# A fused attention and gated-MLP kernel: one more unit of score tiles early, the output projection spread over 36 steps

## The chip, the cores and the metric

The kernel runs on one core of a Trainium2 chip. Its engines are TensorE (PE, with PEld for its weight loads), VectorE (DVE), ScalarE (ACT), GpSimd (POOL) and SyncE (SP), which issues most DMAs. The metric is the device time of one execution in microseconds (us). All floats are 32 bits wide.

## The reference

With 2048 tokens, model width 512, 32 heads of 16 and a hidden width of 1376, the program computes

```
xn = layernorm(x)
q, k, v = split(xn @ wqkv)                      # 32 heads of 16
s = softmax(q @ k.T / 4) @ v                    # per head
s = concat_heads(s) @ wo
g = gelu_tanh(xn @ w1 + b1) @ w2 + b2
out = x + s * silu(g)
```

## The kernel before, in words

Most products are made of three matmuls of a rounded high part and a low remainder (`mm3`, and `i, j` in `terms`). The work has two parts.

**The dense part** makes xn, v, q, k and the MLP. Its matmuls are cut to 64 rows, so that two run beside each other on the two 64-row halves of TensorE ("row tiles", `a` = 0 and 1). `run` issues them alternately and calls `fill` ahead of each. `fill` adds score tiles. A score tile is 128 queries by 512 keys of one head: one matmul of 48 rows (`s_mm`, L193) into a PSUM bank, and one row maximum by DVE (`s_max`, L199). The maxima are wanted because the second pass subtracts them inside its matmul. `fill` makes a tile whenever the count of dense matmuls (`row`) has reached `2 * FILL0 + APART * (tiles made)`, until `SOON` tiles are made. In the dense part the tiles use two banks in turn (`s_ring = [ps_a, ps_b]`), so each tile waits for the maximum of the tile but one before it. A unit is one group of four heads by 512 queries, 64 tiles; when it ends, DVE makes `nm` from its maxima (L255), every second time with a transpose (L244).

POOL makes the low parts (`w_split`, and `hl` at L375, which the second MLP product reads). Its `chore` adds b2 to a finished MLP tile and sends it to DRAM (`g_d`).

**The attention loop** has 32 units of 16 steps, 512 steps and a last one. A step makes the transposed scores of 128 keys by 512 queries for four heads ("T", `t_one`, L716: 4 matmuls of 50 rows on the two row tiles, into banks of `ps_m`, `two`, `two` and `ps_t`), their exponentials on ACT (L719 and L721), and the product with V of the step before ("V", `pv_step`, L787: 4 matmuls on column tiles, each executed as two). Between them stand two or three of the remaining score tiles (letters S, X, Y of `ORDER`; here three banks are in the ring). The letters give TensorE's order by hand. `due(n)` says how many tiles are made by step n; `FEW` takes some away, one each 16 steps until it is used up.

From step `DONE` on no score tile is left. The order `TWO` then holds "H", the projection with Wo of two token tiles (`w_halves`, L916, 6 matmuls of 64 rows on both row tiles, 8 such halves for a pair of token tiles, into two banks of the ring), and "W" (`w_out`): DVE multiplies the finished projection with the gate (`w_gate`, L922), POOL adds x and the result leaves. V is issued for two steps at once there. A token tile's gate is loaded (`load_gx`) and made by a tanh on ACT (L850) and a DVE instruction (L851). After the loop the last six token tiles are projected.

K of a group of four heads lies in one of three sets (`g % KB`); a set is loaded again (`load_k`, on POOL's queue) when its group is done. Units are taken group after group, four chunks of 512 queries each.

Of the kernel before, what the change touches and what calls it, by code (L numbers as in the profile page):

```python
# [16 lines left out]
P = 128  # L17
# [18 lines left out]
DONE = 493  # L36
FILL0 = 2
APART = 5
# [4 lines left out]
TWO = ("HTTTTHWV", "TTTTHHV")  # L43
SOON = 590
FEW = 17
# [3 lines left out]
KB = 3  # L49
XB = 6  # L50
# [4 lines left out]
def fused(ctx: ExitStack, tc: tile.TileContext, x, wqk, wv, wo, w1, b1, w2, b2, out):  # L55
# [45 lines left out]

    s_ring = [ps_a, ps_b]
# [11 lines left out]
    def load_k(g, pieces=range(6), eng=nc.sync, c0=0, n=S):  # L114
        both = kws[g % KB]
        for i in pieces:
            a, b = divmod(i, 3)
            r, cs = slice(64 * a + DH * b, 64 * a + DH * b + DH), slice(c0, c0 + n)
            src = rows((qk_h, qk_h, qk_l)[b], g, 1, a, c0, n)
            if both is not None:  # L120
                eng.dma_start(both[r, :, cs].bitcast(F32), src)
            else:
                for p in range(2):
                    eng.dma_start(kts[g % KB][p][r, cs].bitcast(F32), src[:, p])

# [15 lines left out]
    def q_rows(qs, u, sides=range(2)):  # L141
        g, c = divmod(u, NCH)
# [39 lines left out]
    def at_of(job):  # L182
        u, st, p = job
        return divmod(st, NCH) if u % (NCH * KB) else divmod(st, NCH)[::-1]

    def s_mm(ps, job, a, c0, k0, w):
        u, st, p = job
        qi, ki = at_of(job)
        if u not in MX:
# [4 lines left out]
                                kts[u // NCH % KB][p][r, k0:k0 + w], start=True, stop=True).ins  # L194
# [364 lines left out]
    def fill(a):  # L559
        due = 2 * FILL0 + APART * sum(made)  # L560
        if sum(made) < SOON and row[0] >= due and (made[0] <= made[1]) == (a == 0):
# [4 lines left out]
            s_one(a)  # L566
# [86 lines left out]

    def chore():
# [50 lines left out]
    def t_one(u, k, i, pair=False):  # L705
        g = u // NCH
# [9 lines left out]
        nc.tensor.matmul(ps, kts[g % KB][p][r, k * P:(k + 1) * P],  # L716
# [7 lines left out]
    for n, e in enumerate(plan):  # L724
# [17 lines left out]
        if e[0] == "half" and pairs[e[1]][0] == ("q", NG - 1, 0) and e[2] == 1:  # L742
            kts.append([slot(p, (P, S), F32R) for p in range(2)])
            kws.append(None)
            qss.append(slot(2, (P, 2, 2, CH), F32R))
            ask_k(2)
# [3 lines left out]
    while errands:  # L750
        errand()
    assert sum(made) == SOON
# [12 lines left out]
    wo_h = kp.tile([P, KT, D], F32R, name="wo_h")  # L765
    wo_l = kp.tile([P, KT, D], F32R, name="wo_l")

    WR = {}

    def load_wo(k):  # L770
        WR[k] = wb.tile([P, 2, D], F32, name="gx", bufs=4)[:, 0]
        nc.sync.dma_start(WR[k], wo[k * P:(k + 1) * P, :])

    def wo_high(k):
        nc.gpsimd.tensor_copy(wo_h[:, k], WR[k])

    def wo_low(k):
        nc.gpsimd.tensor_sub(wo_l[:, k], WR.pop(k), wo_h[:, k].bitcast(F32))

    PV, OS, DN, DR = {}, {}, {}, {}  # L780
    def pv_step(u, k):
        g = u // NCH
# [16 lines left out]
    def o_rows(u, j):  # L799
        g, c = divmod(u, NCH)  # L800
# [23 lines left out]
    def o_div(u, eng):  # L824
        g, c = divmod(u, NCH)
# [5 lines left out]
    def home(i):  # L831
        if i not in homes:
            homes[i] = (slot(i, (P, KT, D)) if i < KB else
                        keep_r.tile([P, 2 * KT, D], F32, name="kt0"))
        return homes[i]

    def load_gx(t):
        i = 2 * (t % NCH)
        if t < NW - 2:
            GX[t] = wb.tile([P, 2, D], F32, name="gx", bufs=4)  # L840
        elif t < NT - NCH:
            GX[t] = home(KB)[:, i:i + 2]
# [34 lines left out]
    def w_mul(t, ks, parts=(0, 1)):  # L877
# [4 lines left out]
        for i, cs in enumerate(cols(t)):  # L882
            if i in parts:
                for k in ks:
                    mm3(PW[t][i][:, :cs.stop - cs.start], OTS[t, k], (wo_h[:, k, cs], wo_l[:, k, cs]),
                        k == 0, k == KT - 1)

    def w_two(t, k0):
# [4 lines left out]
        if t:  # L893
            nc.scalar.activation(hi, src, AF.Copy)
        else:
            nc.gpsimd.tensor_copy(hi, src)
# [7 lines left out]
    def w_halves(t, k, side):  # L904
# [7 lines left out]
        for n, (x, y) in enumerate(((0, 0), (0, 1), (1, 0))):  # L912
            for a in range(2):
                i = ts[a ^ side]
                r = slice(64 * a, 64 * a + 64)
                HALF[0] = nc.tensor.matmul(PW[i][0], OTS[i, k][x][r], (wo_h, wo_l)[y][r, k],  # L916
# [27 lines left out]

    for u in range(NU):
        g, c = divmod(u, NCH)
        if c == 0 and g == KB:
            for i in range(6):
                at(52 + i // 2, load_k, g, (i,), nc.gpsimd, 0, CH)
                at(56 + i // 2, load_k, g, (i,), nc.gpsimd, CH, CH)  # L950
                at(64 + i // 2, load_k, g, (i,), nc.gpsimd, S // 2, S // 2)
        elif c == 0 and g > KB:
            for i in range(6):
                at(64 * (g - KB + 1) + 6 + i, load_k, g, (i,), nc.gpsimd)
# [13 lines left out]
    for t in range(NW):  # L968
        n = DONE + 4 * (t // 2)
        at(n - 3 + t % 2, load_gx, t)  # L970
        if t % 2 == 0:
            for i in range(2):
                at(n + i - 2 if t else n + 2 * i - 7, w_two, t, 2 * i)
            for i in range(4):
                for j in range(2):
                    at(n + i, w_halves, t, i % 2 * 2 + j, i // 2, pos="H")
        at(n + t % 2, gate, t)
        at(n + 3, w_out, t, nc.gpsimd, pos="W")
    for i, t in enumerate(late):
        n = L - 2 * len(late) - 1 + 2 * i  # L980
        at(n - 4, load_gx, t)
        at(n, gate, t)
    for i, t in enumerate(late[:2]):
        at(L - 2 + i, w_token, t)
    for k in range(KT):
        at(104 + 16 * k, load_wo, k)
        at(110 + 16 * k, wo_high, k)
        at(114 + 16 * k, wo_low, k)
    jobs.extend(heads[made[0]:])
    since = {}  # L990
    for n in range(L + 1):
# [9 lines left out]
        order = TWO[n % 2] if n >= DONE else ORDER[want] if n > 1 else ("TTTTV", ORDER[2])[n]  # L1001
        if want == 3 and ka == 0:
            order = FIRST
        for op in order:
# [15 lines left out]
            else:  # L1020
# [4 lines left out]
                i += 1  # L1025
    o_move(NU - 1)
# [54 lines left out]
```

## Time and profile before

| | |
|---|---|
| runs before, median | 1546.75 us (1546.65 to 1546.99, 3 runs) |
| profiled execution, first to last instruction | 1544.6 us |
| PE, PEld busy | 1538.4 us (100%), 922.5 us (60%) |
| DVE, ACT, POOL busy | 1419.2 us (92%), 1212.4 us (78%), 375.8 us (24%) |
| DMA | 116.83 MB, mean 76 GB/s |
| granted TensorE clock | 1.000 |

The page gives the profiled execution by its span; the median of the runs is 2.15 us above this span. A busy share of an engine counts the time in which at least one of its instructions was under way. PE's is 100% because neighbouring matmuls overlap in the record, so it does not tell how densely they stand: for that the number of matmuls in a stretch is used.

### The profile page before, as it was taken

How to read it: one execution, taken by the hardware profiler on the slowest of the kernel's cores; microseconds unless marked ns; L12 is line 12 of the kernel's file. 1: busy time of each engine (PE TensorE's matmuls, PEld its weight loads, DVE VectorE, ACT ScalarE, POOL GpSimd, SP SyncE). 2: the span in 40 equal slices, each digit the busy share in tenths (PEclk: the TensorE clock that was granted, in tenths of full speed). 3: DMA queues.
4: the chain of work that ended last, by engine and by line, in shares of the span. 5: the costliest groups of instructions: out<-in, count | busy, mean ns of one | idle time of the engine just before them, and what ended most of it. 6: DMA issues, size and time to landing. Idle time of an engine off the chain costs nothing.

```text
span 1544.6 us, 31302 instructions
## 1 busy us (share of the span) xinstructions
PE 1538.4 (100%) x12230; PEld 922.5 (60%) x12230; DVE 1419.2 (92%) x2294; ACT 1212.4 (78%) x1881; POOL 375.8 (24%) x386
## 2 busy tenths in 40 slices
PE   9999999999999999999999999999999999999998
PEld 8899999999995444444444444444444444444456
DVE  7799999999998999999999999999999999999945
ACT  4333433333339999999999999999999999999994
POOL 4235575756741011001000100100010000000153
PEclk9999999999999999999999999999999999999999
DMA  6615443455422112112411411411051111110162
GB/s 212 155 58 145 124 143 108 120 161 136 141 90 66 39 45 61 33 37 51 75 28 33 71 33 41 60 44 29 21 84 29 32 32 30 41 32 20 50 217 100
DMA packets 78227, 116.83 MB, mean 76 GB/s; under 512 B 28132, under 2 KB 28388, under 8 KB 76904
## 3 DMA queue, kind: packets, MB, share of 16 engines
q1 hardware_dynamic: 73596, 99.80, 23.1%
q0 software_dynamic: 4000, 14.45, 5.0%
q8 instruction: 96, 1.57, 0.4%
q10 hardware_dynamic: 484, 0.60, 0.1%
q14 instruction: 51, 0.42, 0.1%
HBM read 84.35 MB, written 25.97 MB: 71 GB/s over the span
## 4 chain that ended last, share of the span: by engine, by line
PE 99%; DVE 1%; DMA 0%; issue 0%; ACT 0%; DVEq 0%
PE pv L787 33%; PE ps L193 22%; PE ps L583 13%; PE two L716 8%; PE sp L583 5%; PE ps L716 4%; PE pst L716 4%; PE pst L583 3%; PE pv L583 2%; PE ps L916 2%; PE ps L92 1%; PE ps L455 1%; PE pst L92 0%; DVE st L414 0%; PE two L92 0%; DMA xt<-in_x 0%
## 5 line engine op out<-in xcount | busy, mean ns | idle before, releaser
L199 DVE TENSOR_REDUCE mx<-ps 128x2 f32<-128x512 f32 x2048 | 1318.0, 687 | 68.5 <-PE ps L193 18.3
L787 PE MATMUL pv<-slot,vsb 128*32 128x512 f32 x4096 | 543.4, 604 | 0.0
L721 ACT ACTIVATE slot<-two 128x1024 f32<-128x1024 f32 x511 | 520.5, 1019 | 0.0
L193 PEld LDWEIGHTS ps<-kt,slot 48*128 48x128 f32 x1356 | 212.2, 184 | 290.2 <-DVE mx L199 278.4
L193 PE MATMUL ps<-kt,slot 48*128 48x256 f32 (+1 forms) x1356 | 376.3, 366 | 0.0
L719 ACT ACTIVATE slot<-ps 128x512 f32<-128x512 f32 x515 | 307.5, 598 | 16.7 <-PE ps L716 7.2
L719 ACT ACTIVATE slot<-pst 128x512 f32<-128x512 f32 x511 | 309.9, 606 | 0.0
L583 PE MATMUL ps<-slot,w1h 64*128 64x512 f32 x1088 | 225.4, 392 | 0.0
L193 PE MATMUL ps<-kt,qz 48*128 48x512 f32 x512 | 202.2, 395 | 0.0
L716 PE MATMUL two<-qt,kt 50*128 50x512 f32 x766 | 197.5, 395 | 0.3 <-DVE gt L643 0.3
L716 PE MATMUL ps<-qt,kt 50*128 50x512 f32 x387 | 189.7, 492 | 0.0
L193 PEld LDWEIGHTS ps<-slot,slot 48*128 48x128 f32 x590 | 92.8, 184 | 124.0 <-DVE mx L199 118.2
L193 PE MATMUL ps<-slot,slot 48*128 48x256 f32 (+1 forms) x590 | 165.8, 366 | 0.0
L787 PEld LDWEIGHTS pv<-slot,vsb 128*32 128x32 f32 x4096 | 81.5, 108 | 131.9 <-issue 124.4
L583 PEld LDWEIGHTS ps<-slot,w1h 64*128 64x128 f32 x1088 | 154.1, 185 | 9.8
L583 PE MATMUL ps<-slot,w1l 64*128 64x512 f32 x544 | 157.0, 392 | 0.0
L716 PE MATMUL pst<-qt,kt 50*128 50x512 f32 x383 | 155.7, 406 | 0.0
L375 POOL TENSOR_TENSOR hl<-hg,hh 128x512 fp32r<-128x512 f32 x76 | 96.7, 1295 | 158.2 <-ACT hh L374 109.3
L368 ACT ACTIVATE hg<-ps,b_sb 128x512 f32<-128x512 f32 x44 | 27.9, 684 | 133.0 <-PE ps L583 121.7
L716 PEld LDWEIGHTS two<-qt,kt 50*128 50x128 f32 x766 | 114.5, 186 | 1.1 <-DVE gt L643 0.7
L246 POOL CAST mh<-nt 128x32 fp32r<-128x32 f32 x19 | 4.0, 209 | 375.7 <-DVE nt L244 322.8
L193 PEld LDWEIGHTS ps<-kt,qz 48*128 48x128 f32 x512 | 93.7, 183 | 1.0 <-DVE mx L199 0.7
(197 smaller groups left out, 1974.6 us busy)
## 6 DMA issues: line engine op xcount, KB each, us to landing
raw<-in_w SPq DMA_DIRECT2D x88, 256.0 KB
qk_h<-hh SPq DMA_DIRECT2D x32, 256.0 KB
qk_l<-hl SPq DMA_DIRECT2D x32, 256.0 KB
qt<-qk_h SPq DMA_DIRECT2D x128, 64.0 KB
slot<-qk_h SPq DMA_DIRECT2D x92, 64.0 KB
g_d<-gt POOLq DMA_DIRECT2D x16, 256.0 KB, 3.3
qt<-qk_l SPq DMA_DIRECT2D x64, 64.0 KB
dn<-den_d SPq DMA_DIRECT2D x32, 128.0 KB
```

What stands on the lines that cost most here:

```text
L92: nc.tensor.matmul(ps, lhs[a], rhs[b], start=first and n == 0, stop=last and n == 2)
L193: return nc.tensor.matmul(ps[:, c0:c0 + w], QS[u][r, p, qi * P:(qi + 1) * P], kts[u // NCH % KB][p][r, k0:k0 + w], start=True, stop=True).ins
L199: nc.vector.tensor_reduce(MX[u][:, 2 * p:2 * p + 2, qi, ki][:, heads, parts], ps.rearrange("p (n c) -> p n c", c=HC), axis=AX.X, op=OP.max)
L368: nc.scalar.activation(raw, ph.pop(u), AF.Gelu_apprx_tanh, bias=b1_sb[:, u[2]:u[2] + 1])
L375: nc.gpsimd.tensor_sub(hl, raw, hh.bitcast(F32))
L455: nc.tensor.matmul(pq["q", g, c], W1[g][i][:, k * P:(k + 1) * P], (xh, xl)[j][c][:, k], start=n == 0 and k == 0, stop=n == 2 and k == KT - 1)
L583: i = nc.tensor.matmul(ps, lhs[r], rhs[r], start=first, stop=last).ins
L716: nc.tensor.matmul(ps, kts[g % KB][p][r, k * P:(k + 1) * P], QT[u][r, p, :], start=True, stop=True)
L719: nc.scalar.activation(PT[u, k][:, 2 * p + a, :], ps, AF.Exp, scale=SCALE)
L721: nc.scalar.activation(PT[u, k][:, :2], TP["two"], AF.Exp, scale=SCALE)
L787: nc.tensor.matmul(PV[u][32 * j:32 * j + 32, :], vsb[:, k, h:h + 32], PT[u, k][:, j, :], start=(k == 0), stop=(k == NT - 1))
L916: HALF[0] = nc.tensor.matmul(PW[i][0], OTS[i, k][x][r], (wo_h, wo_l)[y][r, k], start=k == 0 and side == 0 and n == 0, stop=k == KT - 1 and ...
```

## The change

Numbers: `SOON` 590 to 654 (64 more tiles in the dense part), `APART` 5 to 4.51, `DONE` 493 to 477, `FEW` 17 to 31.

- `fill` no longer ties a tile's row tile to the dense matmul that follows; the two row tiles alternate.
- A fourth K set lies where Wo lay. `KOF` gives the set of each group; Wo goes into the first K set from step 328 on.
- From unit 24 on, groups 6 and 7 take turns chunk by chunk (`gc`), so that the tokens of a chunk are complete earlier.
- From step 477 on every odd step has one H, every even step one or (four times, `WIDE`) two; V is issued for two steps at once in even steps. Both parts of the projection's operand are made on POOL (before, ACT made the high part for all pairs but the first). One bank leaves the ring of three: it holds the fourth T of odd steps.
- The gates of token tiles 4 to 11 are finished in the dense part: ACT makes the tanh, POOL a product and a sum (`chore`).

```diff
-APART = 5
+APART = 4.51
-TWO = ("HTTTTHWV", "TTTTHHV")
-SOON = 590
-FEW = 17
+SOON = 654
+FEW = 31
+KOF = (0, 1, 2, 3, 0, 2, 1, 3)
+LAST = 24
+WIDE = (3, 7, 11, 15)
...
+    def gc(u):
+        return divmod(u, NCH) if u < LAST else (LAST // NCH + u % 2, (u - LAST) // 2)
...
     def fill(a):
         due = 2 * FILL0 + APART * sum(made)
-        if sum(made) < SOON and row[0] >= due and (made[0] <= made[1]) == (a == 0):
+        if sum(made) < SOON and row[0] >= due:
...
-            s_one(a)
+            s_one(0 if made[0] < made[1] else 1)
...
     def chore():
-        if chores:
+        if turned:
+            gt, rs, e = turned.pop(0)
+            nc.gpsimd.tensor_mul(e, e, gt)
+            nc.gpsimd.tensor_add(gt, gt, e)
+            nc.gpsimd.dma_start(g_d[rs, :], gt)
+        if added:
+            gt, rs = added.pop(0)
+            e = eg[0][:, rs.start // P % NCH]
+            nc.scalar.activation(e, gt, AF.Tanh, scale=0.5)
+            turned.append((gt, rs, e))
+        if chores and (eg or chores[0][1].start < CH):
             gt, rs = chores.pop(0)
             nc.gpsimd.tensor_add(gt, gt, b2_sb)
-            nc.gpsimd.dma_start(g_d[rs, :], gt)
+            if rs.start < CH:
+                nc.gpsimd.dma_start(g_d[rs, :], gt)
+            else:
+                added.append((gt, rs))
...
+        elif i == 3 and u * 16 + k >= DONE and k % 2:
+            ps = TP["odd"].tile([P, CH], F32, name="ps")
...
-    wo_h = kp.tile([P, KT, D], F32R, name="wo_h")
-    wo_l = kp.tile([P, KT, D], F32R, name="wo_l")
+    new_k(kp)
+    k_ones(kts[KB])
...
+    for g in range(KB, NG):
+        free = max([h for h in range(g) if KOF[h] == KOF[g]], default=-1)
+        for i in range(6):
+            at(64 * (free + 1) + 6 + i, load_k, g, (i,), nc.gpsimd)
...
+    halves = [(t, k, side) for t in range(0, NW, 2) for side in range(2) for k in range(KT)]
+    counts, when = {}, []
+    for n in range(DONE, L + 1):
+        counts[n] = 2 if n % 2 == 0 and (n - DONE) // 2 in WIDE else 1
+        when += [n] * counts[n]
+    for i, (n, half) in enumerate(zip(when, halves)):
+        t, k, side = half
+        at(n, w_halves, *half, pos="H")
...
+        if i % 8 == 0 and t + 2 < NW:
+            at(n, w_two, t + 2, 0)
+        if i % 8 == 6 and t + 2 < NW:
+            at(n, w_two, t + 2, 2)
+        if i % 8 == 7:
+            for j in range(2):
+                at(n, w_out, t + j, nc.gpsimd, pos="W")
...
-        order = TWO[n % 2] if n >= DONE else ORDER[want] if n > 1 else ("TTTTV", ORDER[2])[n]
+        if n == DONE:
+            TP["odd"] = s_ring.pop(0)
+        if n >= DONE:
+            order = "TTTTHWV" if n % 2 else "H" * counts[n] + "WTTTTV"
+        else:
+            order = ORDER[want] if n > 1 else ("TTTTV", ORDER[2])[n]
```

TensorE's order in the dense part, in the second MLP product (`run`): `ps<-kt,qz` are score tiles, the others dense matmuls. Before:

```order
L193 MATMUL ps<-kt_604,qz_613 128x512
L583 MATMUL sp<-w2h,hh 128x512 x2
L583 MATMUL sp<-w2l,hh 128x512 x2
L583 MATMUL sp<-w2h,hl 128x512
L193 MATMUL ps<-kt_604,qz_613 128x512
L583 MATMUL sp<-w2h,hl 128x512
L583 MATMUL pv<-w2h,hh 128x512
L583 MATMUL pst<-w2h,hh 128x512
L583 MATMUL pv<-w2l,hh 128x512
L583 MATMUL pst<-w2l,hh 128x512
L193 MATMUL ps<-kt_604,qz_613 128x512
```

Five dense matmuls stand between two score tiles, everywhere. The same kind of place in the changed kernel (its line numbers are 5 higher here):

```order
L198 MATMUL ps<-kt_604,qz_613 128x512
L588 MATMUL sp<-w2l,hh 128x512 x2
L588 MATMUL sp<-w2h,hl 128x512 x2
L198 MATMUL ps<-kt_604,qz_613 128x512
L588 MATMUL pv<-w2h,hh 128x512
L588 MATMUL pst<-w2h,hh 128x512
L588 MATMUL pv<-w2l,hh 128x512
L588 MATMUL pst<-w2l,hh 128x512
L588 MATMUL pv<-w2h,hl 128x512
L198 MATMUL ps<-kt_604,qz_613 128x512
```

Now it is four and five in turn: of the 653 gaps 319 have four dense matmuls and 334 have five.

TensorE's order at the change from one pair of token tiles to the next in the loop's end. `ps_20148` and `ps_20149` are the old pair's banks, `ps_20299` and `ps_20300` the new pair's. Before:

```order
L916 MATMUL ps_20149<-wo_h_6885,ol_20012 128x512
L916 MATMUL ps_20148<-wo_h_6885,ol_20012 128x512
L787 MATMUL pv_19825<-slot5_20172,vsb_90 32x512 x4
L787 MATMUL pv_19825<-slot3_20203,vsb_90 32x512 x4
L716 MATMUL ps_20280<-qt1_6876,kt1_113 128x512
L716 MATMUL two_6862<-qt1_6876,kt1_113 128x512 x2
L716 MATMUL pst_20292<-qt1_6876,kt1_113 128x512
L916 MATMUL ps_20299<-wo_h_6885,oh_20214 128x512
```

Two V products and one T lie between the pairs. In the changed kernel, between the second pair (`ps_20028`, `ps_20029`) and the third (`ps_20228`, `ps_20229`), with what the instruction waits for behind it:

```order
L937 MATMUL ps_20029<-kt0_15864,oh_20012 128x512
L937 MATMUL ps_20028<-kt0_15864,oh_20012 128x512
L937 MATMUL ps_20029<-kt0_15864,ol_20013 128x512
L937 MATMUL ps_20028<-kt0_15864,ol_20013 128x512
L937 MATMUL ps_20228<-kt0_15864,oh_20052 128x512 [waits DVE_49,Pool_49]
L937 MATMUL ps_20229<-kt0_15864,oh_20052 128x512 [waits DVE_49]
L937 MATMUL ps_20228<-kt0_15864,oh_20052 128x512
```

Nothing lies between the pairs here: the ring has two banks left, so the new pair writes the banks that DVE has to read first (`w_gate` of the old pair). Of the four changes of pair three are of this kind (steps 484, 491 to 492, and 505 to 506); at the fourth (498 to 499) T, two V and T lie between.

More of the change, by code (lines that the diff above doesn't have):

```diff
@@ L751, in fused @@
         errand()
+    assert not chores and not added and not turned
     assert sum(made) == SOON
@@ L832, in home @@
         if i not in homes:
-            homes[i] = (slot(i, (P, KT, D)) if i < KB else
-                        keep_r.tile([P, 2 * KT, D], F32, name="kt0"))
+            homes[i] = slot(i, (P, KT, D))
         return homes[i]
```

89 lines of the change are left out of this document (39 added, 50 removed).

## The prediction

> **What bounds the kernel now.** I read the page's shares and chain first, then busy time by stage, then the timelines of the three stages that the change touches.
>
> ```profile
> PE 1538.4 (100%) x12230; PEld 922.5 (60%) x12230; DVE 1419.2 (92%) x2294; ACT 1212.4 (78%) x1881; POOL 375.8 (24%) x386
> PE 99%; DVE 1%; DMA 0%; issue 0%; ACT 0%; DVEq 0%
> 42.30:465.40 423.10, 423.10 (x3582) 393.11 (x3581) 403.36 (x604) 148.98 (x269) 236.02 (x203) 1.00 0.44 125
> 465.40:1466.00 1000.60, 1000.29 (x7869) 447.08 (x7866) 944.59 (x1559) 988.28 (x1483) 84.73 (x124) 1.00 0.20 43
> 1466.00:1521.80 55.80, 55.80 (x462) 33.31 (x462) 25.30 (x29) 51.08 (x84) 29.63 (x30) 1.00 0.53 176
> 1521.80:1544.60 22.80, 18.88 (x102) 14.61 (x100) 13.62 (x21) 2.80 (x5) 6.27 (x5) 0.99 0.31 105
> ```
>
> The last four rows are the stretch with early score tiles, the loop up to step 493, the loop's end, and what follows it; columns are length, then busy time and count of PE, PEld, DVE, ACT and POOL. PE is on the chain throughout, but what holds PE differs by stage.
>
> *Dense part.* These rows give its pace and the ring of two banks. The first is of 60 to 450 us; then one unit's end, one instruction a row.
>
> ```profile
> 60.00:450.00 390.00, 390.00 (x3341) 363.95 (x3338) 379.88 (x569) 138.76 (x251) 228.54 (x195) 1.00 0.42 124
> L199 DVE TENSOR_REDUCE mx<-ps x557: 647/692/695, 59.4 to 449.4; 128x2 f32<-128x512 f32 x186
> ...
> 276.88 0.69 DVE L199 TENSOR_REDUCE mx<-ps 128x2 f32<-128x512 f32 x1
> 276.90 0.18 PEld L193 LDWEIGHTS ps<-kt,qz 48*128 48x128 f32 x1
> 277.12 0.40 PE L193 MATMUL ps<-kt,qz 48*128 48x512 f32 x1
> 277.49 0.28 DVE L255 TENSOR_REDUCE nm<-mx 128x16 f32<-128x128 f32 x1
> 277.63 0.18 PEld L193 LDWEIGHTS ps<-kt,qz 48*128 48x128 f32 x1
> 277.69 0.68 DVE L199 TENSOR_REDUCE mx<-ps 128x2 f32<-128x512 f32 x1
> 278.42 0.18 PEld L193 LDWEIGHTS ps<-kt,qz 48*128 48x128 f32 x1
> 278.52 0.40 PE L193 MATMUL ps<-kt,qz 48*128 48x512 f32 x1
> 278.96 0.69 DVE L199 TENSOR_REDUCE mx<-ps 128x2 f32<-128x512 f32 x1
> ```
>
> 390 us hold 3341 matmuls: 0.1167 us each, so one slot of a row tile is 0.233 us. They hold 557 score tiles: 0.700 us each, which is 5 dense matmuls and the tile at 0.1167. PE is the bound here. But the ring is right behind: the maximum of 276.88 ends at 277.57 and the weights of the tile after next are loaded at 277.63; that of 277.69 ends at 278.37, the load follows at 278.42. A tile's weight load starts 0.05 us after its bank is read out. In the usual case the load is 0.22 us ahead of its matmul (276.90, 277.12). Here DVE was late, by the 0.28 us instruction at 277.49; the lead shrank to 0.10 us (278.42, 278.52), and the maximum still started at 278.96: two tiles, from 277.69, in 1.27 us instead of 1.40.
>
> *Loop.* V starts are the steps' marks; the windows count the `two` exponentials, one a step.
>
> ```profile
> 850.35 1.06 PE L787 MATMUL pv<-slot,vsb 128*32 128x512 f32 x8
> 852.36 1.06 PE L787 MATMUL pv<-slot,vsb 128*32 128x512 f32 x8
> 854.37 1.07 PE L787 MATMUL pv<-slot,vsb 128*32 128x512 f32 x8
> 856.36 1.07 PE L787 MATMUL pv<-slot,vsb 128*32 128x512 f32 x8
> ...
> 599.60:987.50 387.90, 195.48 (x192) 1.00 0.22 45
> 1019.80:1442.40 422.60, 211.75 (x208) 1.00 0.15 35
> ```
>
> A step with three score tiles takes 2.01 us, the one with two (854.37 to 856.36) 1.99: taking a tile out of a step gains almost nothing. In the first window `FEW` leaves out one tile each 16 steps: 387.90 / 192 = 2.020 us a step. In the second it no longer does: 422.60 / 208 = 2.032.
>
> *Loop's end.* One pair of steps:
>
> ```profile
> 1486.25 0.40 PE L716 MATMUL ps<-qt,kt 50*128 50x512 f32 x1
> 1487.51 1.92 PE L787 MATMUL pv<-slot,vsb 128*32 128x512 f32 x16
> 1489.37 0.50 PE L716 MATMUL ps<-qt,kt 50*128 50x512 f32 x1
> 1489.94 0.40 PE L916 MATMUL ps<-wo_h,oh 64*128 64x512 f32 x2
> 1490.63 0.39 PE L916 MATMUL ps<-wo_h,oh 64*128 64x512 f32 x2
> 1492.03 0.40 PE L716 MATMUL ps<-qt,kt 50*128 50x512 f32 x1
> ```
>
> 5.78 us (1486.25 to 1492.03) hold two T, two V and four H. An H is 0.70 us (1489.94 to 1492.03 are three, 2.09). Without H the pair is 5.78 - 2.79 = 2.99, or 1.50 a step.
>
> **The change, part by part.** The sum is made against the profiled execution (span 1544.6 us); the median of the runs, 1546.75, is 2.15 above it, which lies outside first and last instruction and stays.
>
> *64 more tiles in the dense part.* Streaming them costs 64 x 0.1167 = **+7.5 us**. Dense matmuls stay the same.
>
> *The ring at the new pace.* Tiles alternate between row tiles and between banks, so a bank's next tile comes on the same row tile. Between them that row tile has 6 slots always before (1.40 us); now the gaps of four and five make it 5 and 6 slots in turn, 1.17 and 1.40. The ring needs 1.27 by the rows above. A second unit's end, with a transpose, drove it further:
>
> ```profile
> 142.99 0.65 DVE L199 TENSOR_REDUCE mx<-ps 128x2 f32<-128x512 f32 x1
> 143.33 0.39 PE L583 MATMUL pv<-w2l,hh 64*128 64x512 f32 x1
> 143.51 0.40 PE L583 MATMUL pst<-w2h,hl 64*128 64x512 f32 x1
> 143.69 0.18 PEld L193 LDWEIGHTS ps<-kt,qz 48*128 48x128 f32 x1 [0.22 <-DVE mx L199]
> 144.03 0.39 PE L583 MATMUL pv<-w2h,hl 64*128 64x512 f32 x1
> 144.23 0.69 DVE L199 TENSOR_REDUCE mx<-ps 128x2 f32<-128x512 f32 x1
> ```
>
> From 142.99 to 144.23 is 1.24 us, with the load waiting. So a 5-slot stretch is 0.07 to 0.10 us too short; I take 0.087. The 319 short gaps make 160 such stretches on either row tile; those of the two overlap, so I count one set: 160 x 0.087 = **+14 us**. Bounds: 0, if a lead still shorter than any seen costs nothing, and, if two tiles go on to take 1.40, (654 - 590) x 0.700 = 44.8 in place of 7.5 + 14. I take the value near the rows, since the ring was seen to give way to 1.24 and no further. Behind the waiting tile stand all dense matmuls, as PE's order is fixed. The late DVE instruction at a unit's end cost no time when the ring had 0.13 us to spare; ten unit ends without it: **+1 us**.
>
> Whether a waiting tile holds one row tile or both is what the second fence shows too: the pv stream, 0.23 us apart, goes from 143.33 to 144.03 while the score tile is awaited. The Trainium skill ("TensorE: Matmul & The Clock Gate", Part 3, The mechanism) has it that matmuls start and end strictly in program order, and only weight loads are pulled ahead. The trace agrees here with its 0.70 us. What this rule can do to the sum is a rival below.
>
> *Gates in the dense part.* Eight tanh on ACT and sixteen POOL operations:
>
> ```profile
> L375 POOL TENSOR_TENSOR hl<-hg,hh 128x512 fp32r<-128x512 f32 x76 | 96.7, 1295 | 158.2 <-ACT hh L374 109.3
> L850 ACT ACTIVATE slot<-gx 128x512 f32<-128x512 f32 x8 | 5.2, 650 | 0.0
> L922 DVE SCALAR_TENSOR_TENSOR gx<-ps,gx 128x512 f32<-128x512 f32 x8 | 5.1, 679 | 3.6 <-PE ps L916 3.6
> ```
>
> 16 x 1.295 = 20.7 us go to POOL, which is busy 228.54 of 390, and 5.2 to ACT (138.76 of 390). Nothing of it is on PE's path: **0**. Cover: idle POOL time ahead of `hl`. If it fails, each of eight chores can hold an `hl`, and the MLP matmuls that read it, by 2.6: at most 20 us; PE has no such wait today, and I keep 3 of it for the range. What leaves the loop's end (tanh and DVE products) lay beside PE: 0.
>
> *Sixteen steps turn from 2.03 to 1.50 us.* Steps 477 to 492 lose their score tiles, their V is issued by twos, and the 40 H are spread instead of added. 16 x (2.032 - 1.495) = **-8.6 us**.
>
> *One step with two tiles each 16 steps* up to 477 rather than about 272: 204 x (2.032 - 2.020) = **-2.4 us**.
>
> *Two banks for H.* At three changes of token pair the new H follows the old at once, and needs both banks read. PE stands from the last matmul's slot to its end (0.40 - 0.23 = 0.17), then two `w_gate` (2 x 0.68), and a load again (0.05 + 0.10): 1.7 us. Behind it are H, T and V; ACT then waits for T. 3 x 1.7 = **+5.0 us**. Bounds: 0, if ACT were the one awaited there, to 6 with DVE's own work in front. ACT is busy 51.08 of 55.80 us there, with all gates; at 2.2 us a step T may find `two` not yet read: **+0.5** (0 to 3).
>
> *K and Wo moved.* K of group 3 is loaded at step 6 instead of 52, that of group 5 at 198 with its first tile now at about step 214 instead of 236. Sixteen steps are 32 us for twelve DMAs on POOL's queue, whose next waiting work is a division after step 207: **0**; if late, PE stands once for a few us.
>
> Sum: 7.5 + 14 + 1 - 8.6 - 2.4 + 5.0 + 0.5 = **+17.0**, span 1561.6, median **1563.7 us**, 1.1% slower.
>
> **Rivals.**
> - *The ring gives way* (the tile's lead may fall to nothing without loss): 17 - 15 = +2, 1548.7 us; without the stops at the banks 1543.7. For it: no end of the shrinking lead is proved. Against: the 0.22 us wait at 143.69.
> - *The loop gains more*, faster than before: its mean of 2.026 is above the best steps, because DVE falls behind (it now has one tile less in 16 steps) or K comes late (it now comes early). If all 476 steps fell to 2.00, they would gain 476 x 0.026 = 12 in place of 2.4: with a free ring 1539 us. It decides only if the ring costs less than about 5. Against: the step with two tiles still took 1.99.
> - *Both row tiles' waits add*, by program order as above: the 5-slot stretches of the two do not overlap, 28 instead of 14: 1577.7 us.
> - *The ring stays at 1.40*: +44.8 instead of 22.5, 1586 us. Against: 1.24 and 1.27 above.
>
> **How the numbers follow.** Forecast 0.52; ring gives way 0.15; loop gains more 0.15; waits add 0.11; ring stays 0.07. Two runs of this kernel differ by far less than 0.2% (3.1 us), which I take as no change. Faster: the third case and a little of the second, 0.18. Same: the rest of the second, 0.12. Slower: 0.70. The forecast's own range is 1556 to 1572; the range to hold 8 in 10 leaves out the last case and part of the third: **1540 to 1580**.
>
> **What would show it.** In the windows of the changed profile: score tiles in the dense part at 0.667 us (forecast), 0.642 (ring gives way) or 0.70 (ring stays), and waits of PE's weight load for DVE L204 where there were 0.9 us. The last early tile ends 22 us later than at 465.4. From step 1 to 477 at 2.02 a step; then pairs of steps of 4.4 and 5.1 us, with three stops of 1.7 at L937. Wrong would be: a dense part less than 10 us longer, no wait at L937, or POOL's `hl` awaited by PE.

## The result

The changed kernel takes 1573.14 us (median of 4 runs, 1572.77 to 1573.24), the kernel before 1546.70 (4 runs, 1546.49 to 1546.99): a ratio of 1.017, 95% interval 1.0158 to 1.0182. It is slower by 26.4 us, where the forecast was 17.0 us slower (1563.7 us, range 1540 to 1580). The sign and the range held; the size of the loss did not. The profiled span grew from 1544.6 to 1571.3 us, by 26.7.

The page of the changed kernel looks as before at first sight: the engines' shares, and the shares of the chain of waits.

```profile
PE 1559.2 (99%) x12200; PEld 916.0 (58%) x12200; DVE 1398.0 (89%) x2286; ACT 1207.9 (77%) x1873; POOL 395.0 (25%) x398
PE 94%; POOL 2%; DVE 2%; DMA 1%; issue 1%; SPq 0%; ACT 0%; DVEq 0%; POOLq 0%
```

PE is still busy for 99% of the span, but the chain now has 2% of POOL, which is not in the chain of before, and 2% of DVE. The busy times by stage say where. For both kernels the boundaries are the start of the last early tile's maximum, and then the `two` exponentials of steps 477 and 511. First the changed kernel; columns are length, then busy time and count of PE, PEld, DVE, ACT and POOL, the granted clock, and the DMA share.

```profile
42.30:495.21 452.91, 450.81 (x3649) 393.96 (x3649) 433.04 (x671) 154.17 (x279) 257.17 (x221) 1.00 0.41 118
495.21:1461.11 965.90, 965.38 (x7588) 430.73 (x7586) 905.60 (x1493) 956.79 (x1437) 79.23 (x114) 1.00 0.21 44
1461.11:1546.32 85.21, 82.26 (x639) 41.84 (x637) 13.59 (x20) 71.50 (x112) 32.52 (x34) 1.00 0.40 123
1546.32:1571.30 24.98, 20.46 (x110) 15.04 (x106) 13.83 (x21) 4.82 (x9) 7.35 (x6) 1.00 0.28 96
```

The same stages of the kernel before (its first, 42.30 to 465.40, stands in the prediction):

```profile
465.40:1434.43 969.03, 968.72 (x7620) 433.18 (x7617) 914.55 (x1510) 957.14 (x1436) 82.35 (x122) 1.00 0.20 43
1434.43:1519.36 84.93, 84.93 (x690) 45.52 (x690) 55.34 (x78) 80.14 (x128) 30.68 (x32) 1.00 0.42 135
1519.36:1544.60 25.24, 21.32 (x122) 16.31 (x118) 13.62 (x21) 4.88 (x9) 7.60 (x6) 1.00 0.29 98
```

The whole loss is in the dense part: 452.91 - 423.10 = **+29.8 us** (forecast +22.5). The loop up to step 477 gives back 3.1 (forecast 2.4). The end from step 477 on, from which the forecast had 3.1 us back, gives nothing: up to step 511 it is 85.21 against 84.93, and the rest gives 0.3. Together: 29.8 - 3.1 + 0.3 - 0.3 = 26.7.

In the dense part a matmul takes 452.91 / 3649 = 0.1241 us where it took 423.10 / 3582 = 0.1181. The waits of PE's weight loads there (engine, tile and line waiting, for whom: total us, times, longest) explain little of the 22 us that this makes:

```profile
PEld sp L588 <- POOL w2l L300: 3.1, 3, 1.4
PEld ps L198 <- DVE mx L204: 3.0, 9, 0.6
```

The ring's loss does not stand there, because it hides inside PE's busy time. These are the early tiles' rows in a stretch without other stops:

```profile
206.83 4.00 DVE L204 TENSOR_REDUCE mx<-ps 128x2 f32<-128x512 f32 x6
...
207.03 0.39 PE L198 MATMUL ps<-kt,qz 48*128 48x512 f32 x1
...
207.58 0.18 PEld L198 LDWEIGHTS ps<-kt,qz 48*128 48x128 f32 x1
...
207.58 0.49 PE L198 MATMUL ps<-kt,qz 48*128 48x512 f32 x1
...
208.20 0.18 PEld L198 LDWEIGHTS ps<-kt,qz 48*128 48x128 f32 x1
...
208.20 0.50 PE L198 MATMUL ps<-kt,qz 48*128 48x512 f32 x1
...
209.08 0.40 PE L198 MATMUL ps<-kt,qz 48*128 48x512 f32 x1
```

Two tiles have no lead at all: load and matmul start together (207.58, 208.20), and the matmul's record stretches from 0.39 to 0.50 us. This is no exception: from 60 to 480 us 303 of 620 tiles start together with their load; in the kernel before it is 8 of 556 (60 to 450 us). Six maxima take 4.00 us, some 0.66 a tile, where PE's own pace would be 0.642. Over all early tiles from 60 to 480 us the starts of a maximum and of the next but one lie 1.35 us apart on average: 222 of 620 below 1.32 (mean 1.29), 178 from there to 1.37, 202 from there to 1.42, and 18 above.

### The profile page after: what moved, and what is told of

Its sections match the earlier page's. It is cut to its first block, busy times and chain, and to the rows that moved or that the text cites. A ratio compares the mean times of both kernels' runs of the same rounds, so it can differ in the third digit from the quotient of the medians.

```text
span 1571.3 us, 31218 instructions
## 1 busy us (share of the span) xinstructions
PE 1559.2 (99%) x12200; PEld 916.0 (58%) x12200; DVE 1398.0 (89%) x2286; ACT 1207.9 (77%) x1873; POOL 395.0 (25%) x398
## 4 chain that ended last, share of the span: by engine, by line
PE 94%; POOL 2%; DVE 2%; DMA 1%; issue 1%; SPq 0%; ACT 0%; DVEq 0%; POOLq 0%
PE pv L814 32%; PE ps L198 21%; PE ps L588 11%; PE two L738 8%; PE pst L738 5%; PE ps L738 5%; PE sp L588 4%; PE pst L588 2%; PE pv L588 2%; PE ps L937 2%; PE ps L460 1%; PE ps L94 0%; POOL w2l L300 0%; POOL hl L380 0%; PE pst L94 0%
## 5 line engine op out<-in xcount | busy, mean ns | idle before, releaser
L741 ACT ACTIVATE slot<-ps 128x512 f32<-128x512 f32 x533 | 317.3, 598 | 22.8 <-PE ps L738 9.1
L741 ACT ACTIVATE slot<-pst 128x512 f32<-128x512 f32 x493 | 299.1, 607 | 0.0
L198 PE MATMUL ps<-kt,qz 48*128 48x512 f32 x512 | 227.4, 444 | 0.0
L738 PE MATMUL ps<-qt,kt 50*128 50x512 f32 x405 | 193.0, 485 | 0.0
L198 PE MATMUL ps<-slot,slot 48*128 48x512 f32 (+1 forms) x566 | 170.5, 376 | 0.1
L588 PE MATMUL ps<-slot,w1l 64*128 64x512 f32 x544 | 153.2, 392 | 0.0
L738 PE MATMUL pst<-qt,kt 50*128 50x512 f32 x365 | 148.2, 406 | 0.0
L738 PEld LDWEIGHTS ps<-qt,kt 50*128 50x128 f32 x405 | 72.7, 183 | 35.0 <-ACT slot L741 26.8
```

The source lines that it names most:

```text
L198: return nc.tensor.matmul(ps[:, c0:c0 + w], QS[u][r, p, qi * P:(qi + 1) * P], kts[KOF[gc(u)[0]]][p][r, k0:k0 + w], start=True, stop=True).ins
L588: i = nc.tensor.matmul(ps, lhs[r], rhs[r], start=first, stop=last).ins
L738: nc.tensor.matmul(ps, kts[KOF[g]][p][r, k * P:(k + 1) * P], QT[u][r, p, :], start=True, stop=True)
L741: nc.scalar.activation(PT[u, k][:, 2 * p + a, :], ps, AF.Exp, scale=SCALE)
```

## The experiments

The table has the median time of each variant and its stages: the start of the last early tile's maximum, then the length from step 1 to 477, from 477 to 511, and from there to the end (all by the `two` exponentials of the profiled execution, us). Three kernels whose dense part is that of the changed kernel (changed, three_banks, half_two) end it at 495.2, 494.4 and 495.5, so differences under 1 us there mean nothing.

| kernel | time | last early tile | 1-477 | 477-511 | rest |
|---|---|---|---|---|---|
| before | 1546.7 | 465.4 | 964.1 | 84.9 | 25.2 |
| changed | 1573.1 | 495.2 | 961.2 | 85.2 | 25.0 |
| half_max | 1555.2 | 477.5 | 961.3 | 85.3 | 24.7 |
| late_gates | 1580.8 | 492.0 | 961.1 | 95.6 | 25.7 |
| half_late | 1562.0 | 472.5 | 961.2 | 96.1 | 25.8 |
| tiles_590 | 1564.7 | 470.6 | 963.9 | 99.2 | 24.9 |
| before_gates | 1552.3 | 470.0 | 964.2 | 84.9 | 26.1 |
| before_gates_1by1 | 1554.0 | 471.5 | 964.3 | 84.9 | 25.8 |
| three_banks | 1573.9 | 494.4 | 961.2 | 86.4 | 24.7 |
| few_spread | 1549.4 | 465.6 | 966.6 | 84.9 | 25.2 |
| chores_in_pieces | 1570.6 | 492.6 | 961.2 | 85.3 | 25.0 |
| row_swap | 1575.2 | 497.4 | 961.1 | 85.4 | 25.1 |
| half_two | 1570.8 | 495.5 | 961.2 | 83.0 | 24.4 |
| late_gates_after_w | 1572.7 | 492.8 | 961.4 | 86.7 | 25.6 |

### The ring: half_max

```diff
-SCALE = DH ** -0.5
+SCALE = DH ** -0.5 / 4
...
-ps.rearrange("p (n c) -> p n c", c=HC)
+src = ps.rearrange("p (n c) -> p n c", c=HC)
+if "seen" in prog:                 # dense part
+    src = src[:, :, :HC // 2]
```

> The changed kernel, but the maxima of the early tiles are taken over 128 of each 256 columns (and the softmax temperature is divided by four, so that no exponential overflows). This shortens what holds a score bank, and nothing else on the dense part's path. Theory 1, the ring of two banks (bank read out, load, matmul, maximum: 1.27 to 1.28 us in the changed kernel's rows, against 1.17 us of slots) costs the dense part some 15 to 20 us: a tile goes at PE's own 0.642 us instead of 0.677, the last early tile starts at 474 to 480 us instead of 495.2, the time is 1553 to 1559 us. Theory 2, the extra time is not the ring's (PE's own order, or POOL's late W2 parts): last early tile at 490 or later, 1568 us or more.

The last early tile starts at 477.5, 17.7 us earlier; the time is 1555.2 us, and no other stage moves. Theory 1 holds. In the timeline of the dense part of this run:

```profile
207.07 0.42 DVE L207 TENSOR_REDUCE mx<-ps 128x2 f32<-128x256 f32 x1 [0.26 <-PE ps L198]
207.31 0.39 PE L198 MATMUL ps<-kt,qz 48*128 48x512 f32 x1
207.74 0.42 DVE L207 TENSOR_REDUCE mx<-ps 128x2 f32<-128x256 f32 x1 [0.24 <-PE ps L198]
...
208.02 0.40 PE L198 MATMUL ps<-kt,qz 48*128 48x512 f32 x1
...
208.47 0.40 PE L198 MATMUL ps<-kt,qz 48*128 48x512 f32 x1
...
209.18 0.39 PE L198 MATMUL ps<-kt,qz 48*128 48x512 f32 x1
...
209.87 0.40 PE L198 MATMUL ps<-kt,qz 48*128 48x512 f32 x1
```

With a maximum of 0.42 us DVE waits for PE, and the five- and six-slot stretches of the forecast lie bare: 207.31 to 208.47 is 1.16 us, 208.02 to 209.18 is 1.16, 208.47 to 209.87 is 1.40. With the full maximum each short one takes 1.28 or a little more, so it loses about 0.12; the forecast's 160 of them make 19 us. The gain measured is 17.7 here, and 19.5 with the gates out of the dense part as well (492.0 in late_gates against 472.5 in half_late, both below).

This run shortens DVE's work along with the ring, so alone it does not tell a slow ring from a DVE at its limit. The changed kernel's rows do. In its short stretches a load starts 0.05 us after the read-out, and most maxima start 0.04 us after the end of their matmul: DVE waits for the ring. And where DVE is behind in the loop, maxima of the same size start 0.60 us apart (582.44, 583.05 and 583.65), less than the 0.677 a tile of the dense part. A third bank in the dense part, which would change the ring alone, was not run.

### POOL: late_gates and half_late

```diff
 def chore():
-    if turned:
-        gt, rs, e = turned.pop(0)
-        nc.gpsimd.tensor_mul(e, e, gt)
-        nc.gpsimd.tensor_add(gt, gt, e)
-        nc.gpsimd.dma_start(g_d[rs, :], gt)
...
+    if chores:
+        gt, rs = chores.pop(0)
+        nc.gpsimd.tensor_add(gt, gt, b2_sb)
+        nc.gpsimd.dma_start(g_d[rs, :], gt)
...
+if i % 8 == 7 and t + 2 < NT - NCH:
+    for j in range(2):
+        if t + 2 + j >= NCH:
+            at(n, gate, t + 2 + j)
```

> The changed kernel, but the gates of token tiles 4 to 11 are not made in the dense part: its chores do what they did before (add b2, store), and the loop's end makes the eight gates. Theory 1, the chores' product and sum on POOL (1.3 us each) make w_split's low part of W2 late, and PE waits for it: the waits of PE's weight load for POOL L300 vanish, the last early tile starts 3 to 5 us earlier (490 to 492), and the loop's end, which gets eight tanh back, is 0 to 3 us longer: 1569 to 1572 us. Theory 2, these waits come from elsewhere: the dense part stays within 1 us, and the time is 1573 or more.

> Both edits, half the columns in the early maxima and the gates of tiles 4 to 11 back in the loop's end. If ring and POOL are all that lengthens the dense part beside PE's streaming of 64 tiles (7.5 us), the last early tile starts at 473 us (465.4 + 7.5), give or take 1.5, and the time is 1550 to 1555 us. If something else is in it, the last early tile starts at 477 or later.

In the dense part both went as theory 1 has it: the waits for POOL vanish, the last early tile starts 3.2 us earlier beside the ring and 4.9 us earlier without it. With ring and gates both gone it starts at 472.5, and its rows are PE at its old pace, 430.24 / 3651 = 0.1178 us:

```profile
42.30:472.54 430.24, 430.24 (x3651) 405.41 (x3651) 281.01 (x671) 149.53 (x271) 237.04 (x205) 1.00 0.44 124
```

What made PE wait shows in POOL's timeline of the changed kernel: product, sum, store and addition of one chore (422.19 to 426.98, 4.8 us; the store takes 0.57 after 0.30 of waiting), then `hl`, then the low part of W2,

```profile
422.19 1.28 POOL L664 TENSOR_TENSOR slot<-slot,gt 128x512 f32<-128x512 f32 x1
423.55 1.29 POOL L665 TENSOR_TENSOR gt<-gt,slot 128x512 f32<-128x512 f32 x1
425.14 0.57 POOL L666 DMA_DIRECT2D g_d<-gt  x1 [0.30 <-POOL gt L665]
425.73 1.32 POOL L674 TENSOR_TENSOR gt<-gt,b_sb 128x512 f32<-128x512 f32 x1
426.98 2.55 POOL L380 TENSOR_TENSOR hl<-hg,hh 128x512 fp32r<-128x512 f32 x2
429.47 1.28 POOL L300 TENSOR_TENSOR w2l<-raw,w2h 128x512 fp32r<-128x512 f32 x1
```

and PE's weight load of that part, from PE's own timeline, when it ends:

```profile
430.80 0.19 PEld L588 LDWEIGHTS sp<-w2l,hh 64*128 64x128 f32 x2 [1.35 <-POOL w2l L300]
```

So the 29.8 us are 7.1 for streaming 64 tiles, 17.7 for the ring and 4.9 for the gates, with the ring taken away first; with the gates taken away first, they are 3.2 and the ring 19.5. Both times, though, missed: the loop's end is 10.4 us longer. That was my order, not the gates' work: in these runs two gates stand ahead of `w_gate` in DVE's order, and wait for their tanh while PE waits for `w_gate`. PE's timeline of late_gates has the row

```profile
1496.63 1.72 PE L923 MATMUL ps<-kt,oh 64*128 64x512 f32 x4 [3.73 <-DVE gx L929]
```

The next run puts them behind it.

### Gates, in the right order: late_gates_after_w

```diff
-if i % 8 == 7 and t + 2 < NT - NCH:
-    at(n, gate, t + 2 + j)
+if i % 8 == 1 and t >= NCH:
+    at(n + j, gate, t + j)
+if i == len(halves) - 1:
+    at(n, gate, NW + j)
```

> The changed kernel with the gates of tiles 4 to 11 back in the loop's end, as in the run late_gates, but each gate stands behind the w_gate of the token pair before it in DVE's order (one step after it), not ahead of it. Theory 1, ACT is what pairs of steps wait for in the changed loop's end (4.50 of 4.61 us), so eight tanh of 0.65 us add 3 to 6 us there: from step 477 to 511 88 to 91 us instead of 85.2, dense part 3.2 us shorter, time 1573 to 1576. Theory 2, they lie beside PE there as they did in the kernel before, and the 10.4 us of late_gates was its order on DVE alone: 85 to 86.5 us, time 1570 to 1571.

Between the two: 86.7 us from 477 to 511, 1.5 longer, and 0.6 more after it, against 2.5 us less in the dense part. The spans are 1571.2 and 1571.3. Gates in the dense part neither gain nor lose in the changed kernel.

### Gates alone: before_gates and before_gates_1by1

```diff
 # the kernel before, with chore() of the changed kernel, and
-at(n + t % 2, gate, t)
+if t < NCH:
+    at(n + t % 2, gate, t)
-at(n, gate, t)
+if t in T3:
+    at(n, gate, t)
```

> The kernel before with one part of the change alone: the gates of token tiles 4 to 11 are made by the dense part's chores, as in the changed kernel, and no longer in the loop's end. Theory 1, the loop's end of before is held by ACT nearly as much as by PE (PE's weight loads wait 8.4 us for ACT there): the dense part ends 3 to 5.5 us later than 465.4, as in the run with 590 tiles (470.6), the loop's end is 3 to 8 us shorter: 1542 to 1549 us. Theory 2, the forecast's own step, what leaves the loop's end lay beside PE and gains nothing: 1549.5 to 1552.5 us.

1552.3 us, ratio 1.0032 (1.0021 to 1.0044): theory 2. The dense part is 4.6 us longer, the loop's end exactly as long (84.9): what left it had lain beside PE, as the forecast said. The dense part's loss is two stops, at 338 and 408 us, where two matmuls start 1.87 and 1.84 us apart. Its waits name the same part of W2:

```profile
PEld sp L583 <- POOL w2l L295: 4.7, 4, 1.9
```

```diff
 if turned:
-    gt, rs, e = turned.pop(0)
-    nc.gpsimd.tensor_mul(e, e, gt)
-    nc.gpsimd.tensor_add(gt, gt, e)
-    nc.gpsimd.dma_start(g_d[rs, :], gt)
+    gt, rs, e, summed = turned[0]
+    if not summed:
+        nc.gpsimd.tensor_mul(e, e, gt)
+        turned[0] = gt, rs, e, True
+    else:
+        nc.gpsimd.tensor_add(gt, gt, e)
+        nc.gpsimd.dma_start(g_d[rs, :], gt)
+        turned.pop(0)
...
-{4: [lambda: w1_split(j + 1)], 8: [errand], 10: [chore]}
+{4: [lambda: w1_split(j + 1)], 6: [chore], 8: [errand], 10: [chore]}
```

> As the run before it, but a chore gives POOL one operation at a time (1.3 us) instead of up to three at once (3.9 us), with twice as many chores. Theory 1, PE waits for POOL in the dense part because up to 3.9 us of chores stand ahead of w_split's low part in POOL's order: the dense part ends 0 to 2 us later than 465.4, and the time is 2 to 5 us below the run before it. Theory 2, any POOL operation added there costs, however it is placed: the same time as the run before it, within 1 us.

Neither theory. The two stops are gone, but a new one stands earlier, at 203 us, and it costs 5.9: with twice as many places, four additions of `b2` with their stores come within 10 us, and now `hl` is late (PE waits 2.8 us for POOL L375). The dense part ends 6.1 us later.

### Pieces without crowding: chores_in_pieces

```diff
-        elif chores and (eg or chores[0][1].start < CH):
+        elif own and chores and (eg or chores[0][1].start < CH):
...
-{4: [lambda: w1_split(j + 1)], 6: [chore], 8: [errand], 10: [chore]}
+{4: [lambda: w1_split(j + 1)], 6: [lambda: chore(False)], 8: [errand], 10: [chore]}
```

This is the edit of before_gates_1by1, in the changed kernel, with `own` false at the new places: a call there begins no addition.

> The changed kernel, with chores in smaller pieces: the old places start one b2 addition each or do one POOL operation of a gate; new places, halfway between, only go on with gates already begun, so that no b2 additions and stores crowd together. Theory 1, PE's stops in the dense part come from POOL work that is bunched (in the run with one operation at a time the two old stops were gone, and the one new stop, at 203 us, stood behind four additions with their stores): no stop for POOL is left, the last early tile starts 4 to 5.5 us earlier than 495.2, the time is 1567 to 1569 us. Theory 2, POOL lacks the time for eight gates wherever they stand: PE's waits for POOL stay at 2 us or more and the time at 1571 or more.

No wait of PE for POOL is left in the dense part, so theory 1 has the cause; but the gain is 2.6 us (492.6, 1570.6 us), short of the 4 to 5.5. Beside the ring a stop costs less than its length, as the 3.2 of late_gates already said: I had taken the 4.9 that holds without the ring.

### The ring's parity: row_swap

```diff
-s_one(0 if made[0] < made[1] else 1)
+s_one((1, 0, 0, 1)[sum(made) % 4])
```

> The changed kernel, but the early tiles go to the row tiles in the order 1 0 0 1 instead of 1 0 1 0, so that a bank's next tile comes on the other row tile. Theory 1, the ring loses because a bank's next tile on the same row tile meets five and six slots in turn (1.17 and 1.40 us) while it needs 1.28: on the other row tile each stretch is near 5.5 slots, 1.28 us, and most of the 17 us goes: the last early tile starts at 478 to 486, the time is 1556 to 1564 us. Theory 2, the slots of the two row tiles start nearly together (0.02 to 0.2 us apart), so the stretches stay near five and six whatever the row tile: the last early tile within 3 us of 495.2, 1570 to 1576 us.

497.4 and 1575.2 us: theory 2. The dense part's waits have 40 loads that wait for a maximum, where the changed kernel has 9:

```profile
PEld ps L198 <- DVE mx L204: 8.0, 40, 0.6
```

The other row tile does not make the stretches even: from 60 to 480 us 182 of 616 are below 1.30 us and 89 above 1.42, where the changed kernel has 175 and 18 of 620.

### The number of tiles: tiles_590

```diff
-DONE = 477
+DONE = 493
-APART = 4.51
+APART = 5
-SOON = 654
+SOON = 590
-FEW = 31
+FEW = 17
-counts[n] = 2 if n % 2 == 0 and (n - DONE) // 2 in WIDE else 1
+counts[n] = 2
...
-order = "TTTTHWV" if n % 2 else "H" * counts[n] + "WTTTTV"
+order = "TTTTHHWV" if n % 2 else "HHWTTTTV"
```

> The changed kernel with the old number of early tiles: 590, one in five slots, one tile left out each 16 steps until 17 are, paired V from step 493, and two H in each of the last 20 steps; the fourth K set, the chunk order, the two H banks and the gates in the dense part stay. If the change's loss lies in the 64 tiles, the dense part ends near 466 to 469 us and the time is 1546 to 1552 us. Rival, that the parts that stay here (K order, two banks for H, gates early) cost most of it: 1558 us or more.

The dense part does as theory 1 says but for the gates: 470.6, 24.6 us earlier than with 654 tiles, and 5.2 later than before. The time does not: 1564.7 us, because the loop's end takes 99.2. With two H in every step my schedule asks for `w_two` too late, and PE waits for POOL's `oh` and `ol` (its waits from 1471 to 1538 us):

```profile
PE ps L937 <- POOL oh L917: 6.2, 4, 1.6
PE ps L937 <- POOL ol L918: 3.1, 4, 1.0
```

After two of these stops PE's clock is also at half for 3.41 us each (from 1488.2 and from 1532.5). That is this run's own doing, and it says nothing on the banks or on the K order in the last steps.

### Banks: three_banks

```diff
-elif i == 3 and u * 16 + k >= DONE and k % 2:
-    ps = TP["odd"].tile([P, CH], F32, name="ps")
...
-if n == DONE:
-    TP["odd"] = s_ring.pop(0)
```

> The changed kernel, but the H ring keeps its third bank, and the fourth T of the odd steps goes back to the bank that it has in the even ones. Theory 1, the three stops at L937 come from two banks: with a third, the next pair's first H needs one bank only, each stop shrinks from about 1.5 to 0.7 us or less, and T loses nothing: the loop's end is 2 to 4 us shorter, 1569 to 1571 us. Theory 2, the odd bank is what lets T run ahead of its exponentials: the pairs of steps grow from 4.61 to 4.8 us or more, which takes away what the stops gain: 1573 us or more.

Theory 2. The stops shrink by 0.6 us each: the first one's step takes 3.63 us instead of 4.20. But a plain pair of steps grows from 4.61 to 4.87, since the fourth T waits for its exponential. 1573.9 us; the two choices are worth the same.

### What holds the last 35 steps: half_two

```diff
+n = 1 if u * 16 + k >= DONE else 2
+if n == 1:
+    nc.vector.memset(PT[u, k][:, 1], 1.0)
-nc.scalar.activation(PT[u, k][:, :2], TP["two"], AF.Exp, scale=SCALE)
+nc.scalar.activation(PT[u, k][:, :n], TP["two"][:, :n], AF.Exp, scale=SCALE)
```

> The changed kernel, but from step 477 ACT makes the exponential of only one of the two score blocks in the bank pair named two; DVE, which is idle there, writes ones for the other, so half of those probabilities are left out. Theory 1, a plain pair of steps takes 4.61 us instead of the 4.4 of PE's work because ACT has 2 x (1.03 + 2 x 0.61) = 4.50 us in it and T waits for a bank to be read: with 0.4 us a step less on ACT, pairs fall to 4.40, the loop from step 477 to 511 from 85.2 to 81 to 82.5 us, the time to 1569 to 1571 us. Theory 2, the 4.61 is PE's own: the pairs stay at 4.6 and the time within 1 us of 1573.

Plain pairs fall from 4.61 to 4.38 us, which is the forecast's 4.4; the stage falls by 2.2 to 83.0, and the time to 1570.8. The pairs do what theory 1 says; the stage falls a little short of its numbers, since pairs with a stop stay as they were. ACT's groups in the changed kernel (1461 to 1546 us) show why:

```profile
L743 ACT ACTIVATE slot<-two 128x1024 f32<-128x1024 f32 x34 | 35.0, 1030 | 0.0
L741 ACT ACTIVATE slot<-ps 128x512 f32<-128x512 f32 x52 | 30.2, 604 | 13.7 <-PE ps L738 7.7 <-PE pst L738 6.0
```

A step needs 1.03 + 2 x 0.61 us of ACT, a pair 4.5, and this is above the 4.4 that PE needs. In a pair's timeline of the changed kernel, the T of the second step start as the exponential of the first step's `two` ends (1490.99 + 1.02 = 1492.01):

```profile
1490.99 1.02 ACT L743 ACTIVATE slot<-two 128x1024 f32<-128x1024 f32 x1
...
1491.70 0.40 PE L937 MATMUL ps<-kt,ol 64*128 64x512 f32 x2
...
1492.06 0.51 PE L738 MATMUL two<-qt,kt 50*128 50x512 f32 x2
```

### The left-out tiles: few_spread

```diff
-min(FEW, n // 16)
+min(FEW, n // 28)      # in the kernel before
```

> The kernel before, with its 17 left-out score tiles one in 28 steps over the whole loop instead of one in 16 up to step 272. Theory 1, the gain of 0.012 us a step comes from DVE catching up, and one tile in 28 steps is enough: steps 273 to 477 fall from 2.032 to 2.021 us, the first 272 stay within 0.002 of 2.020, and the time is 2 to 3 us shorter, 1544 to 1545 us. Theory 2, the gain is what the left-out tiles themselves save and goes with their number: the loop's length stays, 1546.5 to 1547 us.

Neither. It is slower, 1549.4 us, ratio 1.0015 (1.0005 to 1.0024). Steps 17 to 273, and then 273 to 477, of the kernel before and, below, of this run:

```profile
502.70:1019.96 517.26, 517.26 (x4068) 229.97 (x4067) 487.51 (x803) 512.62 (x770) 51.68 (x78) 1.00 0.23 46
1019.96:1434.43 414.47, 414.47 (x3267) 185.13 (x3266) 394.73 (x656) 408.53 (x613) 24.64 (x37) 1.00 0.15 36
```

```profile
502.94:1022.79 519.85, 519.85 (x4084) 232.05 (x4083) 490.20 (x810) 512.70 (x770) 51.66 (x78) 1.00 0.24 46
1022.79:1437.09 414.30, 414.30 (x3251) 184.63 (x3250) 390.22 (x648) 408.53 (x613) 24.67 (x37) 1.00 0.16 36
```

The first stretch loses its whole gain, the second gains nothing although tiles are left out in it. The starts of `two`, averaged by a step's place in its unit, show where the gain is: with a tile out at step 0 of a unit, steps 15, 0 and 2 take 2.01, 2.00 and 2.09 us; with three tiles there they take 2.05, 2.09 and 2.15. The other thirteen steps differ by less than 0.03. What is gained is a unit's start, 0.18 us each, by a tile left out just there, and not by fewer tiles.

## Why the prediction was right, and where it was wrong

- **64 tiles, +7.5**: right. 7.1 us (half_late).
- **The ring, +14 and +1**: right in mechanism, too small. A five-slot stretch loses about 0.12 us, not 0.087, and the ring took 17.7 (the +1 for unit ends was not measured apart). The step that failed is "the ring was seen to give way to 1.24 and no further": it took two of the eight shortest intervals in the trace of before (1.23 to 1.27) as the ring's period. Both stood behind a stall, and the 1.24 has a maximum of 0.65 us in it; in steady work the same ring takes 1.28 to 1.30, with the weight load 0.05 us behind the read-out, no lead, some 0.53 us to the maximum, and 0.69 for it. This sum could have been made from the rows of before. The waits of the two row tiles overlap, as the sum had it: the rival by which they add, 28 us, is out.
- **Gates in the dense part, 0**: wrong by 4.9 us, inside the "at most 20" of its bound. The cover that I named, idle POOL time ahead of `hl`, was an average (228.54 busy of 390); chores come in bunches of 4.8 us. I also watched for `hl` alone. In the changed kernel the part that comes late is the low part of W2, behind it in the same queue.
- **What leaves the loop's end, 0**: right for the kernel before (before_gates). In the changed one it is worth 1.5 to 2.1 us (late_gates_after_w).
- **One tile in 16 steps, -2.4**: 2.9 measured, right in size; its cause is the unit's start, which the forecast did not name. The rival by which all steps fall to 2.00 is out: steps that are not at a unit's start stay at 2.01 to 2.02.
- **Three stops at L937, +5.0**: right. The two pairs of steps that hold the first two stops and three H take 6.70 and 6.73 us where a pair with three H and no stop takes 5.08; the pair with the third takes 6.07 where 4.40 was due: 1.6, 1.6 and 1.7 us. The row is

```profile
1476.92 1.23 PE L937 MATMUL ps<-kt,oh 64*128 64x512 f32 x4 [0.88 <-DVE gx L943]
```

- **T finds `two` not yet read, +0.5**: mis-sized, 2.2 us (half_two), inside its bound of 3. The forecast set ACT's busy share of the stage beside PE's and did not add up ACT's work in one pair: 4.5 us against the 4.4 that it gave the pair.
- **Sixteen steps at 1.50, -8.6**: with 4.9 for stops and 2.2 for T the stage should be 1.5 us shorter, and it is 0.3 longer. About half of the 1.8 between is a matter of counting: the forecast has 40 H in the end of either kernel, but between steps 477 and 511 the changed kernel has 228 projection matmuls and the kernel before 220, and 8 x 0.117 is 0.9 us. Of the rest, 0.7 us are two pairs that take 4.73 and 4.71 even in half_two (steps 487 to 488 and 501 to 502), where the others are at 4.4. Why they do, and why the time after step 511 does not become 0.9 us shorter in return (25.2 to 25.0), stays open.

Of the rivals, "the ring gives way" would have put the tiles at 0.642 us, "stays at 1.40" at 0.70; they went at 0.677 with the POOL stops and at 0.672 without them (late_gates). Three terms were too low at once (the ring by 2.7 us, the gates by 4.9, the last stage by 3.4); the others were within 0.7. So the time is inside the range because the range was wide, not because misses cancelled.

No variant beats the kernel before. The two measured repairs of the changed kernel's own terms are worth 2.5 us (chores_in_pieces) and nothing (late_gates_after_w); 17.7 us hang on a maximum that takes 0.69 us a tile and a ring of two banks.

## What to carry to other kernels

A ring at its limit can be missing from the list of waits (3.0 of 17.7 us stood there): look for a weight load and its matmul with one start, and compare the period of the slowest loop through a bank (read-out, load, matmul, reduction) with the slots it is given, using steady rows and not the shortest ones. Work put on an engine that is half idle is priced by the longest bunch ahead of the instruction that someone awaits, and not by its mean load. Where two engines need nearly the same time in one pair of steps (4.4 and 4.5 us here), removing work from one of them gains only up to the other.

## What the runs showed of the hardware

**A short stop of PE can halve its clock afterwards.** In late_gates the last matmul before the stop ends at 1492.89. The windows around it (columns as above, with the granted clock before the DMA share and GB/s):

```profile
1493.00:1494.00 1.00, 0.00 (x0) 0.00 (x0) 0.00 (x0) 1.00 (x3) 0.00 (x0) 1.00 0.64 238
1494.00:1495.00 1.00, 0.00 (x0) 0.00 (x0) 0.42 (x1) 1.00 (x2) 0.00 (x0) 0.77 0.17 66
1495.00:1496.00 1.00, 0.00 (x0) 0.00 (x0) 1.00 (x3) 0.01 (x1) 0.00 (x0) 0.50 0.00 0
...
1500.00:1501.00 1.00, 1.00 (x9) 0.35 (x9) 0.00 (x0) 0.48 (x1) 0.72 (x2) 0.50 0.03 12
1501.00:1502.00 1.00, 1.00 (x12) 0.20 (x12) 0.00 (x0) 1.00 (x3) 0.92 (x2) 0.82 0.68 238
```

The clock falls from 1.00 to 0.50 some 1.6 us after that end (0.77 in the window from 1494 to 1495), and comes back at about 1501.4, 4.7 us after work resumed at 1496.63. The stop in before_gates_1by1 did the same, with 0.50 from 205.9 to 212.7 us: from 208 to 212 us PE has 22 matmuls, where it has 37 from 196 to 200. That is how 3.15 us between two matmuls came to cost 5.9. The stops of 1.87 us in before_gates, and those of the changed kernel, left the clock at 1.00.

A stop's length alone does not decide. In every trace the clock's changes lie whole multiples of 3.41 us apart: half clock lasts 6.83 us in late_gates, half_late and before_gates_1by1, and 3.41 in tiles_590. Cut into such stretches of 3.41 us, the seven falls ahead of a kernel's last 10 us follow stretches in which PE had no matmul for 1.64 us (late_gates, 1491.12 to 1494.53) to 3.07 us (half_late); no stretch at full clock with up to 1.55 us is followed by a fall. The border is not sharp: two stretches near a kernel's end, with 1.66 and 1.70 us, kept the clock. So a stop of 1.55 us was followed by a fall in tiles_590 (1484.44 to 1485.99, fall at 1488.17), where its stretch held 1.85 us in all, and another of 1.54 us (1500.28 to 1501.81) was not. The Trainium skill ("TensorE: Matmul & The Clock Gate", Part 1, What's actually happening) puts the loss of the clock after an idle window of about 3.4 us; the length of the window agrees with these traces, but it need not be idle throughout: 1.64 us in it were enough.

**Maxima overlap on DVE.** Each maximum's record is 0.69 us long, but in the changed kernel's dense part about one in five (117 of 620) starts less than 0.61 us after the one before, so two records overlap by up to 0.09 us. By these starts DVE was not at its limit at 0.677 us a tile.
